# Six edits to an attention, MLP and expert kernel: early decay fills, fp32 partial sums, a fifth block in 128 rows, expert conversions behind the slots

## The chip, the cores and the metric

One NeuronCore of a Trainium2 chip runs the whole kernel. The metric is the device time of one execution in microseconds; lower is better. The engines are TensorE (PE in the profile), VectorE (DVE), ScalarE (ACT), GpSimd (POOL) and SyncE (SP). SP only issues DMAs here; POOL computes a little, issues some DMAs and all gathers and scatters. Each engine takes its instructions in order, so an instruction that waits holds up all that stand behind it on its engine.

## What is computed

Three stages are chained. Attention with a decay term and a causal mask (4 batches, 8 heads, 576 positions, 64 per head), a squared-ReLU MLP over the 2304 tokens, and a mixture of 8 experts of which each token uses two.

```python
scores = np.where(causal, -1e9, q @ k.T / 8 + cum[:, :, :, None] - cum[:, :, None, :])
x = softmax(scores) @ v                         # 4 x 8 x 576 x 64, then (2304, 512)
h = np.maximum(x @ w_in, 0.0)                   # w_in 512 x 2048
x = h * h @ w_out                               # w_out 2048 x 512
noisy = x @ w_gate + np.log1p(np.exp(x @ w_noise)) * noise
# the two largest of 8 per token, softmax of the two as gates
for e in range(8):
    out[mask] += gate * (np.maximum(x[mask] @ w1[e], 0.0) @ w2[e])   # 512 -> 1024 -> 512
```

## The kernel before

Nearly every product is made from fp16 halves: each operand is split into a high and a low fp16 part, and three matmuls (high by high, high by low, low by high) stand for one fp32 product. The splits are work for ACT (high part) and DVE (low part).

**Attention.** The first 256 positions of each batch ("head") are computed in 12 pieces, `hd_s(j, bank)` (L387). A piece fills two PSUM tiles `psab`, one from each half of the 128 rows of the array (z = 0, 1): fp32 products of 64 rows (L398), the decay terms (L403) and the mask (L409). Pieces 0 to 7 are placed by hand; 8 to 11 come from `hd_tick` inside the MLP loop. The other 320 positions ("tail") go in units (batch b, block i, head pair p): scores in `att_s` (L216), the exponential, a split, and `att_pv` (L305), whose probabilities come transposed through DMA. Block i = 4 has only 64 positions. There the two heads of a pair share a PSUM tile (64 columns each), and two kinds of matmul use 64 rows: the mask (L243) and the last of five key blocks in `att_pv` (L323, `K = 64`). There are 16 such units. `prep` (L189) readies the tail's operands in four buffer sets; `make_set` (L173) lets POOL fill the decay rows of a set (`setq`, one memset and two selects, L178 to L180), and `prep` copies three rows of `c16` into `setk` by two DMAs from POOL's queue (L202).

**MLP.** `mm1` (L585, 512 to 2048) and `mm2` (L647, 2048 to 512) run over 6 chunks c of 384 tokens and 16 column blocks i. The weight blocks W[i] arrive as packed words and are unpacked by `conv_w` (DVE L550, L555, L559, ACT L562, DVE L565), so the passes are (c = 0, i 0 to 7), (1, 0 to 7), (0, 8 to 15), (1, 8 to 15), then chunks 2 to 5 whole. Chunks 0 and 1 are therefore left half done: `spill` (L622) writes their PSUM sums `acc` to DRAM as two fp16 halves (ACT, then DVE L626), `unspill` loads them, and `mm2` adds them by two matmuls with `ident2k`, 2048 times the identity (L645), for each of the 3 token tiles.

**Router, slots, experts.** `router` makes the logits of a chunk; `slots` chooses the two experts and a row for each token: a chain of small DVE steps from `lg` (L728) to `si` (L792), then six scatters to `table` on POOL (L795). `slot_rows` reads the rows of an expert back (`tix` on SP, L860, and `gs` on POOL, L862), `gather` fetches their tokens (`xg` on POOL, L871, transposed to `xgT` on SP, L873). `layer1(e)` (L913) and `layer2(e)` (L930) are the expert's two products; its result `y` is scatter-added to the output on POOL (L934). An expert's weights come in 8 loads `wr` of 512 KB on SP into 5 buffers (`fetch_next`), and are split by `split_next` (ACT L835, DVE L836, both 128x1024).

**What sets the order.** A hand-written plan orders all engines up to the first pass of chunk 0. Behind it a scheduler orders each engine's instructions from the program's order and its own estimates; `tc.issue_after(x)` keeps what it encloses behind instruction x.

## Time and profile before

| what | value |
|---|---|
| median of 3 runs | 978.59 us (976.27 to 986.29) |
| the profiled execution | 981.3 us, span of its trace 979.1 us |
| mean granted TensorE clock | 0.983 of full speed |
| PE, DVE, ACT, POOL busy | 944.0, 570.3, 445.6, 209.4 us |
| DMA, mean over the span | 159 GB/s |

The span is the time from the first to the last event of the trace; the execution is 2.2 us longer. Times in rows are microseconds from the span's start unless a column says ns. In a row, `out<-in` names the tiles that an instruction writes and reads, `xN` counts instructions, and `[t <-X]` says that the engine had been idle for t before it and what ended that. The granted clock is a share of TensorE's 2.4 GHz; 0.5 is its lower level of 1.2 GHz.

### The profile page before, as it was taken

The page shows a single profiled execution, that of the slowest core. Times are in us where ns is not written, and L with a number is a line of the kernel's source. Part 1 is how long each engine was busy: PE and PEld are TensorE (multiplying, and loading weights), DVE is VectorE, ACT ScalarE, POOL GpSimd, SP SyncE. Part 2 cuts the span into 40 slices and gives each one's busy share as a digit, 9 for nine tenths or more (in the row PEclk, how much of TensorE's full clock was granted, in tenths as well). Part 3 has the DMA queues.
Part 4 walks back from the last instruction along what each step waited for, and adds up shares of the span by engine and source line. Part 5 has one row for each costly group of instructions (what it writes and reads, how often), then busy time and mean ns, then how long its engine had stood idle before and what let it go on. Part 6 is the DMA issues. An engine that isn't in the chain of part 4 may idle for free.

```text
span 979.1 us, 17623 instructions
## 1 busy us (share of the span) xinstructions
PE 944.0 (96%) x6866; PEld 547.8 (56%) x6866; DVE 570.3 (58%) x1253; ACT 445.6 (46%) x990; POOL 209.4 (21%) x249
## 2 busy tenths in 40 slices
...
GB/s 301 118 242 224 200 149 267 176 215 172 224 156 250 204 89 234 144 55 99 106 332 113 210 37 97 106 219 174 241 144 188 129 194 96 236 82 27 42 12 43
DMA packets 219879, 155.34 MB, mean 159 GB/s; under 512 B 175698, under 2 KB 186322, under 8 KB 217746
## 3 DMA queue, kind: packets, MB, share of 16 engines
...
q10 hardware_dynamic: 144, 0.13, 0.1%
...
## 4 chain that ended last, share of the span: by engine, by line
PE 71%; DMA 8%; issue 7%; DVE 5%; POOL 3%; ACT 2%; SPq 2%; POOLq 0%; DVEq 0%; ACTq 0%
PE e L913 18%; PE e L930 17%; PE m L585 13%; PE acc L647 12%; PE po L320 2%; SPq L873 1%; DMA wr<-in_w_dram 1%; DMA w<-in_w_io_dram 1%; POOL table L795 1%; PE psab L398 1%; PE ps L226 1%; PE ps L227 1%; DMA pt<-phl 1%; PE po L323 1%; DMA xg<-x2d,tix 1%
## 5 line engine op out<-in xcount | busy, mean ns | idle before, releaser
L930 PE MATMUL e<-w2s,hT 128*128 128x512 f16 (+1 forms) x960 | 211.1, 382 | 2.0 <-ACT hT L917 1.3
L913 PE MATMUL e<-xgT,w1s 128*128 128x310 f16 (+2 forms) x1536 | 207.7, 297 | 4.1 <-DMA xgT<-xg 4.1
L647 PE MATMUL acc<-w,g 128*128 128x512 f16 x864 | 205.4, 380 | 0.0
L913 PEld LDWEIGHTS <-w1s 128*128 128x128 f16 x1536 | 140.3, 98 | 70.3 <-issue 8.2
L585 PE MATMUL m<-xT,w 128*128 128x384 f16 x960 | 173.7, 331 | 4.9 <-ACT r L592 3.7
L917 ACT ACTIVATE hT<-e 128x310 f16<-128x310 f32 (+2 forms) x128 | 54.7, 428 | 268.2 <-PE e L913 267.9
L930 PEld LDWEIGHTS <-hT 128*128 128x128 f16 (+1 forms) x960 | 99.8, 104 | 110.1 <-issue 2.2
L585 PEld LDWEIGHTS <-w 128*128 128x128 f16 x1152 | 109.9, 99 | 81.0 <-issue 10.4
L647 PEld LDWEIGHTS <-g 128*128 128x128 f16 x864 | 81.0, 98 | 86.2 <-DVE g L603 0.3
L933 DVE TENSOR_SCALAR y<-e,gs 128x512 f32<-128x512 f32 (+1 forms) x40 | 30.0, 750 | 159.3 <-PE e L930 133.8
L918 DVE SCALAR_TENSOR_TENSOR hT<-e,hT 128x310 f16<-128x310 f32 (+2 forms) x128 | 60.6, 477 | 80.7 <-ACT hT L917 80.4
L934 POOL DMA_INDIRECT out_dram<-y,tix x40 | 65.0, 1625 | 169.6 <-DVE y L933 125.1
L795 POOL DMA_INDIRECT table<-ent,si x36 | 41.4, 1149 | 166.0 <-DVE si L792 156.6
L592 ACT ACTIVATE r<-m 128x384 f32<-128x384 f32 x80 | 39.2, 490 | 68.1 <-PE m L585 67.7
L255 DVE TENSOR_REDUCE sm<-ps 128x1 f32<-128x384 f32 (+2 forms) x96 | 53.1, 562 | 22.1 <-PE ps L243 8.7
L871 POOL DMA_INDIRECT xg<-x2d,tix x40 | 44.3, 1108 | 83.6 <-DMA xgT<-xg 73.3
L258 ACT ACTIVATE pr<-ps,sm 128x384 f32<-128x384 f32 (+1 forms) x64 | 40.2, 630 | 25.8 <-DVE sm L257 23.4
L593 ACT ACTIVATE g<-r 128x384 f16<-128x384 f32 x96 | 50.1, 521 | 3.2 <-PE acc L647 1.5
L836 DVE SCALAR_TENSOR_TENSOR w2s<-wr,w2s 128x1024 f16<-128x1024 f32 x32 | 39.1, 1223 | 19.8 <-ACT w2s L835 19.8
L602 DVE TENSOR_TENSOR r<-r 128x384 f32<-128x384 f32 x64 | 35.4, 553 | 25.2 <-ACT g L593 24.9
L836 DVE SCALAR_TENSOR_TENSOR w1s<-wr,w1s 128x1024 f16<-128x1024 f32 x32 | 39.0, 1225 | 12.7 <-ACT w1s L835 12.5
L279 DVE TENSOR_TENSOR phl<-pr,phl 128x384 f16<-128x384 f32 (+1 forms) x64 | 38.5, 619 | 13.2 <-ACT phl L278 12.8
...
## 6 DMA issues: line engine op xcount, KB each, us to landing
...
```

What stands on the lines that cost most here:

```text
L255: seen[u] = nc.vector.tensor_reduce(sm[:, z:z + 1], ps[z][:, :N], AX.X, ALU.max).ins
L585: nc.tensor.matmul(ps, W[i][:, wi, 0, 128 * cc:128 * cc + 128], xT[:, xi, cc, r0:r0 + CH], start=(x == 0), stop=(x == 11))
L593: nc.scalar.activation(g[:, 0, :], r, AF.Square, scale=2.0 ** -10)
L647: last[0] = nc.tensor.matmul(acc[t], g[:, gi, 128 * t:128 * t + 128], W[i][:, wi, 1, :], start=(i in ends[c][0] and x == 0), stop=(i in en ...
L795: s_ = nc.gpsimd.indirect_dma_start(out=table, out_offset=bass.IndirectOffsetOnAxis(ap=si[:, t, k:k + 1], axis=0), in_=ent[:, t, k, :], in ...
L836: nc.vector.scalar_tensor_tensor(lo, t_, sc, hi, op0=ALU.mult, op1=ALU.subtract)
L871: nc.gpsimd.indirect_dma_start(out=xg, out_offset=None, in_=x2d[0:seen, :], in_offset=bass.IndirectOffsetOnAxis(ap=rows_t[key, j][0], axis=0))
L913: last[0] = nc.tensor.matmul(ps[:, :hw], w1s[:, cc, wi, 128 * i:128 * i + 128], xgT[:, 4 * xi + cc, c], start=(x == 0), stop=(x == 11)).ins
L917: relu[0] = nc.scalar.activation(hi, ps[:, :hw], AF.Relu).ins
L918: nc.vector.scalar_tensor_tensor(hT[:, i, 1, c], ps[:, :hw], 0.0, hi, op0=ALU.max, op1=ALU.subtract)
L930: last[0] = nc.tensor.matmul(ps[:m], hT[:, i, hi, 128 * j:128 * j + m], w2s[:, i, wi, :], start=(i == 0 and x == 0), stop=(i == NFE - 1 an ...
L934: s_ = nc.gpsimd.indirect_dma_start(out=out, out_offset=bass.IndirectOffsetOnAxis(ap=ix[:m], axis=0), in_=y[:m], in_offset=None, compute_o ...
```

## The change

Six edits.

1. **Fills.** The decay rows of the sets 0, 1 and 3 are filled by POOL at the start, behind the constants; set 2 stays where it was. The constant `ident2k` goes.
2. **Partial sums.** `spill` writes one fp32 copy made by ACT; the six DVE steps L626 go. `unspill` is one DMA for a chunk, into the buffer of the packed weights (`w64`). The 12 matmuls L645 go. In `x2_out` of chunks 0 and 1, DVE adds the loaded sums to `acc` (6 new steps of 128x512), and the two steps behind it read SBUF instead of PSUM.
3. **Fifth block.** The mask matmul and the last block of `att_pv` use all 128 rows, also for i = 4 (the rows added are zero).
4. **Head pieces.** From piece 8 on, the matmuls of a piece are chained so that the two row halves take turns.
5. **Rows of slots.** `tix` and `gs` get 8 buffers instead of 6.
6. **Conversions.** In the last chunk, the first five expert weight loads stand behind the first store of chunk 4's result; expert 0's 8 conversions stand behind `si` of the slots of chunk 4, and expert 1's 8 conversions go into `layer1(0)`, one behind each ReLU. Before, 12 of the 16 stood in the last pass and 4 behind it, all before `layer1(0)`.

```diff
@@ -168,3 +168,2 @@
 
-    ident2k = consts.tile([128, 128], F16, name="ident2k")
     ones16 = consts.tile([128, 128], F16, name="ones16")
@@ -174,8 +173,12 @@
         KK[n] = apool.tile([128, 2, 2, S], F16, name=f"setk{n}", tag=f"setk{n}", bufs=1)
+        if n not in QQ:
+            with tc.issue_after(pin["pool"]):
+                make_q(n)
+
+    def make_q(n):
         QQ[n] = apool.tile([128, 2, 2, REST], F16, name=f"setq{n}", tag=f"setq{n}", bufs=1)
         q2 = QQ[n][64:70, 1]
-        with tc.issue_after(pin["pool"]):
-            nc.gpsimd.memset(q2, -8.0)
-            nc.gpsimd.affine_select(q2[:, 0], q2[:, 0], [[0, REST]], ALU.is_ge, 0.0, base=2, channel_multiplier=-1)
-            nc.gpsimd.affine_select(q2[:, 1], q2[:, 1], [[0, REST]], ALU.is_ge, 0.0, base=-3, channel_multiplier=1)
+        nc.gpsimd.memset(q2, -8.0)
+        nc.gpsimd.affine_select(q2[:, 0], q2[:, 0], [[0, REST]], ALU.is_ge, 0.0, base=2, channel_multiplier=-1)
+        nc.gpsimd.affine_select(q2[:, 1], q2[:, 1], [[0, REST]], ALU.is_ge, 0.0, base=-3, channel_multiplier=1)
 
@@ -242,3 +245,3 @@
                         r = slice(64 * z, 64 * z + 64)
-                        nc.tensor.matmul(ps[r, 224:288], identw[0:64, 0:64], maskw[0:64, 0:64], start=False, stop=True, skip_group_check=True)
+                        nc.tensor.matmul(ps[r, 224:288], identw[:, 0:64], maskw[:, 0:64], start=False, stop=True, skip_group_check=True)
 
@@ -316,3 +319,2 @@
             vi, pi = HL3[x]
-            K = 128 if kb < 4 else 64
             first, last = kb == 0 and x == 0, kb == i and x == 2
@@ -322,4 +324,4 @@
             else:
-                nc.tensor.matmul(po[64 * h:64 * h + 64, p // 2, 0, p % 2, :], pt[:K, kb, pi, 64 * h:64 * h + 64],
-                                 vs[:K, kb, h, vi, :], start=first, stop=last, skip_group_check=True)
+                nc.tensor.matmul(po[64 * h:64 * h + 64, p // 2, 0, p % 2, :], pt[:, kb, pi, 64 * h:64 * h + 64],
+                                 vs[:, kb, h, vi, :], start=first, stop=last, skip_group_check=True)
         if p == 3:
@@ -391,2 +393,4 @@
         np_ = 4 // (i + 1)
+        v4 = [t.rearrange("p (c w) -> p c w", w=Wd) for t in ps]
+        prods = []
         for p in range(np_):
@@ -397,4 +401,3 @@
                     r = slice(64 * z, 64 * z + 64)
-                    nc.tensor.matmul(ps[z][:, c], hd["x", b, i][r, 1, pp, :], hd["x", b, kb][r, 0, pp, :],
-                                     start=(p == 0 and kb == 0), stop=False, skip_group_check=True)
+                    prods.append((ps[z][:, c], hd["x", b, i][r, 1, pp, :], hd["x", b, kb][r, 0, pp, :], p == 0 and kb == 0, False))
         for p in range(np_):
@@ -402,5 +405,3 @@
                 r = slice(64 * z, 64 * z + 64)
-                nc.tensor.matmul(ps[z][:, Wd * p:Wd * p + Wd], decay(r, 4 * b + np_ * a + p, 128), c16[r, 0:Wd],
-                                 start=False, stop=False, skip_group_check=True)
-        v4 = [t.rearrange("p (c w) -> p c w", w=Wd) for t in ps]
+                prods.append((ps[z][:, Wd * p:Wd * p + Wd], decay(r, 4 * b + np_ * a + p, 128), c16[r, 0:Wd], False, False))
         for hf in range(2):
@@ -408,4 +409,9 @@
                 r = slice(64 * z, 64 * z + 64)
-                nc.tensor.matmul(v4[z][:, :, 128 * i:128 * i + 128], identb[r, hf], masku[r, hf, None, :].to_broadcast([64, np_, 128]),
-                                 start=False, stop=(hf == 1), skip_group_check=True)
+                prods.append((v4[z][:, :, 128 * i:128 * i + 128], identb[r, hf], masku[r, hf, None, :].to_broadcast([64, np_, 128]), False, hf == 1))
+        prev = None
+        for o_, l_, r_, first, end in prods:
+            with ExitStack() as guard:
+                if j >= NPL and prev is not None:
+                    guard.enter_context(tc.issue_after(prev))
+                prev = nc.tensor.matmul(o_, l_, r_, start=first, stop=end, skip_group_check=True).ins
         if a == 0:
@@ -619,3 +625,3 @@
     ends = [((0, NA), (NA - 1, NF - 1)) if c < 2 else ((0,), (NF - 1,)) for c in range(NCH)]
-    part = dram.tile([2 * CH, 2 * DM], F16, name="part")
+    part = dram.tile([2 * CH, DM], F32, name="part")
 
@@ -623,5 +629,4 @@
         for t in range(NT):
-            sp = gpool.tile([128, 2 * DM], F16, name="sp", tag="x2", bufs=3)
-            nc.scalar.activation(sp[:, :DM], acc[t], AF.Copy, scale=2.0 ** -11)
-            nc.vector.scalar_tensor_tensor(sp[:, DM:], acc[t], 2.0 ** -11, sp[:, :DM], op0=ALU.mult, op1=ALU.subtract)
+            sp = gpool.tile([128, DM], F32, name="sp", tag="x2", bufs=3)
+            nc.scalar.activation(sp, acc[t], AF.Copy)
             nc.sync.dma_start(part[CH * c + 128 * t:CH * c + 128 * t + 128, :], sp)
@@ -631,7 +636,4 @@
     def unspill(c):
-        for t in range(NT):
-            if t % 2 == 0:
-                bk = astream.tile([128, 2, 2 * DM], F16, name="bk", tag="pr", bufs=3)
-            back[t] = bk[:, t % 2, :]
-            nc.sync.dma_start(back[t], part[CH * c + 128 * t:CH * c + 128 * t + 128, :])
+        back[c] = astream.tile([128, NT, DM], F32, name="bk", tag="w64", bufs=2)
+        nc.sync.dma_start(back[c], part[CH * c:CH * c + CH, :].rearrange("(t p) d -> p t d", p=128))
 
@@ -642,5 +644,2 @@
                 acc[t] = psM.tile([128, DM], F32, name=f"acc{t}", tag=f"acc{t}", bufs=1)
-            if i == NA + 4 and c < 2:
-                for z in range(2):
-                    nc.tensor.matmul(acc[t], ident2k, back[t][:, DM * z:DM * z + DM], start=False, stop=False)
             for x, (gi, wi) in enumerate(((0, 0), (0, 1), (1, 0))):
@@ -650,2 +649,4 @@
     x2T_t = {}
+    x2_put = [None]
+    slotted = [None]
 
@@ -655,7 +656,11 @@
             x2T = gpool.tile([128, 8, 128], F16, name="x2T", bufs=3)
-            nc.scalar.activation(x2[:, :DM], acc[t], AF.Copy, scale=2.0 ** -10)
-            nc.vector.scalar_tensor_tensor(x2[:, DM:], acc[t], 2.0 ** -10, x2[:, :DM], op0=ALU.mult, op1=ALU.subtract)
+            src = acc[t]
+            if c < 2:
+                src = back[c][:, t]
+                nc.vector.tensor_tensor(src, acc[t], src, op=ALU.add)
+            nc.scalar.activation(x2[:, :DM], src, AF.Copy, scale=2.0 ** -10)
+            nc.vector.scalar_tensor_tensor(x2[:, DM:], src, 2.0 ** -10, x2[:, :DM], op0=ALU.mult, op1=ALU.subtract)
             r0 = SPARE + CH * c + 128 * t
             nc.sync.dma_start_transpose(out=x2T, in_=x2)
-            nc.sync.dma_start(x2d[r0:r0 + 128, :], x2)
+            x2_put[0] = nc.sync.dma_start(x2d[r0:r0 + 128, :], x2).ins
             x2T_t[t] = x2T
@@ -791,3 +796,3 @@
         nc.vector.tensor_reduce(sf, sl, AX.X, ALU.add)
-        nc.vector.tensor_copy(si, sf)
+        slotted[0] = nc.vector.tensor_copy(si, sf).ins
         for t in range(NT):
@@ -858,5 +863,5 @@
         rows = slice(r0, r0 + 128 * n) if row is None else bass.ds(row, 128)
-        tix = epool.tile([128, NJ, 2], I32, name="tix", bufs=6)
+        tix = epool.tile([128, NJ, 2], I32, name="tix", bufs=8)
         nc.sync.dma_start(tix[:, :n, :].rearrange("p j w -> p (j w)"), table[rows, :].rearrange("(p j) w -> p (j w)", p=128))
-        gs = epool.tile([128, NJ], F32, name="gs", bufs=6)
+        gs = epool.tile([128, NJ], F32, name="gs", bufs=8)
         nc.gpsimd.tensor_scalar(gs[:, :n], tix[:, :n, 1].bitcast(F32), 2.0 ** -25, None, op0=ALU.mult)
@@ -1024,5 +1029,7 @@
             nc.gpsimd.memset(half[64:128], 1.0)
-            for t_, cmp, val in ((identw, ALU.not_equal, 1.0), (maskw, ALU.is_ge, -BIG), (ident2k, ALU.not_equal, 2048.0)):
+            for t_, cmp, val in ((identw, ALU.not_equal, 1.0), (maskw, ALU.is_ge, -BIG)):
                 nc.gpsimd.memset(t_, 0.0)
-                pin["pool"] = nc.gpsimd.affine_select(t_, t_, [[-1, 128]], cmp, val, base=0, channel_multiplier=1).ins
+                nc.gpsimd.affine_select(t_, t_, [[-1, 128]], cmp, val, base=0, channel_multiplier=1)
+            for n in (0, 1, 3):
+                make_q(n)
         elif tok[0] == "X" and tok[1] != "T":
@@ -1155,6 +1162,7 @@
         if (c, i) == (NCH - 1, 2):
-            for _ in range(WR):
-                fetch_next()
-        if c == NCH - 1 and i >= 4:
-            split_next()
+            with tc.issue_after(x2_put[0]):
+                for _ in range(WR):
+                    fetch_next()
+        if c == NCH - 1 and 4 <= i < 12:
+            split_next(slotted[0])
         if (c, i) == (NCH - 1, 5):
@@ -1172,6 +1180,10 @@
     ov = ctx.enter_context(tc.tile_pool(name="ov", bufs=1, side="left"))
-    while at["split"] < 16:
-        split_next()
     lastp = []
-    layer1(0, 0, NE0, lambda i: lastp.append(router(NCH - 1, (psE, "e2", 2, 512), last[0])) if i == NR1 else None, last[0])
+
+    def begin(i):
+        split_next(relu[0])
+        if i == NR1:
+            lastp.append(router(NCH - 1, (psE, "e2", 2, 512), last[0]))
+
+    layer1(0, 0, NE0, begin, last[0])
     layer2(0, 0, NE0, lambda j: slots(NCH - 1, lastp[0], (psE, "e2", 2, 512), last[0]) if j == 0 else None)
```

What it moves on the engines is seen at three places (line numbers before and after differ by some: L202 is L205, L795 is L800, L728 is L733, L836 is L841, L398 to L409 are all L416).

On POOL, at about 210 to 235 us: the copies into the four `setk` sets and the first six scatters to `table`. Before:

```order
L202 DMA setk0_1635<-c16_84 3x2x576 x2
L285 MEMSET ph4_2690 128x2x64
L285 MEMSET ph4_2785 128x2x64
L202 DMA setk1_1653<-c16_84 3x2x576 x2
L795 DMA table_82<-ent_2518,si_2550 19456x2 x6
L202 DMA setk2_1719<-c16_84 3x2x576 x2
L202 DMA setk3_1786<-c16_84 3x2x576 x2
```

After:

```order
L205 DMA setk0_1636<-c16_84 3x2x576 x2
L288 MEMSET ph4_2670 128x2x64
L205 DMA setk1_1650<-c16_84 3x2x576 x2
L288 MEMSET ph4_2759 128x2x64
L205 DMA setk2_1712<-c16_84 3x2x576 x2
L800 DMA table_82<-ent_2498,si_2530 19456x2 x6
L205 DMA setk3_1779<-c16_84 3x2x576 x2
```

The copy into set 2 now stands ahead of the six scatters; only that into set 3 is left behind them.

On DVE, the beginning of the chain of `slots` for chunk 4, with the conversions (`w1s`, `w2s`) and the MLP's `r` and `g`. Before:

```order
L728 TENSOR_SCALAR lg<-pl 128x48
L603 SCALAR_TENSOR_TENSOR g<-r,g 128x384
L836 SCALAR_TENSOR_TENSOR w2s<-wr,w2s 128x2x512
L733 TENSOR_SCALAR u__6773<-e__6772 128x24
L736 TENSOR_SCALAR d__6778<-u__6773 128x24
L836 SCALAR_TENSOR_TENSOR w2s<-wr,w2s 128x2x512
L737 TENSOR_TENSOR e__6772<-e__6772,d__6778 128x24
L738 RECIPROCAL u__6773<-u__6773 128x24
L836 SCALAR_TENSOR_TENSOR w2s<-wr,w2s 128x2x512
L739 TENSOR_TENSOR e__6772<-e__6772,u__6773 128x24
L602 TENSOR_TENSOR r<-r 128x384
L740 TENSOR_TENSOR l__6774<-l__6774,e__6772 128x24
```

After:

```order
L733 TENSOR_SCALAR lg<-pl 128x48
L738 TENSOR_SCALAR u__6750<-e__6749 128x24
L741 TENSOR_SCALAR d__6755<-u__6750 128x24
L742 TENSOR_TENSOR e__6749<-e__6749,d__6755 128x24
L743 RECIPROCAL u__6750<-u__6750 128x24
L744 TENSOR_TENSOR e__6749<-e__6749,u__6750 128x24
L745 TENSOR_TENSOR l__6751<-l__6751,e__6749 128x24
L746 TENSOR_TENSOR l__6751<-l__6751,nz 128x24
L748 TENSOR_TENSOR nl<-l__6751,lg 128x24
L752 MAX m_6764<-nl 128x8 x3
L753 MAX_INDEX i_6765<-m_6764,nl 128x8 x2
```

The conversions have left the chain; no conversion stands between `lg` and `si` any more (before, twelve), and four stand right behind `si`.

On PE, the products of head piece 11 (`psab`, two tiles, one for each row half). Before, one half of it, with the other half a hundred rows further on:

```order
L398 MATMUL psab_1304<-hraw_203,hraw_677 128x128
L398 MATMUL psab_1304<-hraw_677 128x128
L398 MATMUL psab_1304<-hraw_203,hraw_677 128x128
L398 MATMUL psab_1304<-hraw_677 128x128
L403 LDWEIGHTS esel_92
L403 MATMUL psab_1304<-c16_84,esel_92 128x256
```

After, both halves (their first product stands 47 rows ahead of these):

```order
L416 MATMUL psab_1309<-hraw_210,hraw_684 128x128
L416 MATMUL psab_1308<-hraw_684 128x128
L416 MATMUL psab_1309<-hraw_684 128x128
L416 MATMUL psab_1308<-hraw_210,hraw_684 128x128
L416 MATMUL psab_1309<-hraw_210,hraw_684 128x128
L416 MATMUL psab_1308<-hraw_684 128x128
L416 MATMUL psab_1309<-hraw_684 128x128
L416 LDWEIGHTS esel_92
L416 MATMUL psab_1308<-c16_84,esel_92 128x256
```

The tiles now alternate, 1205 and 1206, where before one tile's four products followed each other.

## Rows read from the trace of the kernel before

**Rows 1.** The page: busy time of each engine, its share of the span, instructions.
```profile
PE 944.0 (96%) x6866; PEld 547.8 (56%) x6866; DVE 570.3 (58%) x1253; ACT 445.6 (46%) x990; POOL 209.4 (21%) x249
```

**Rows 2.** Windows: stretch, length, busy time of PE, PEld, DVE, ACT, POOL, PEclk, DMA, GB/s.
```profile
100.00:120.00 20.00, 20.00 (x156) 11.90 (x155) 19.16 (x34) 14.84 (x39) 3.21 (x12) 1.00 0.85 177
...
140.00:160.00 20.00, 16.34 (x82) 8.26 (x81) 18.13 (x21) 16.00 (x26) 7.75 (x10) 0.91 0.54 179
...
260.00:480.00 220.00, 220.00 (x2007) 122.15 (x2006) 166.22 (x469) 132.85 (x318) 37.89 (x52) 1.00 0.72 150
```

**Rows 3.** Two waits of PE: what waited, for what, total us, times, longest.
```profile
PE ps L227 <- DMA setk<-c: 1.4, 1, 1.4
...
PE e L930 <- ACT hT L917: 1.3, 1, 1.3
```

**Rows 4.** The chain that ended last, 170 to 175 us: start, us, what.
```profile
172.21 0.43 PE acc L645 x2
```

**Rows 5.** Timeline of PE at 301 us, a unit of block 4: start, us, instructions.
```profile
301.15 0.32 PE L237 MATMUL ps<-setk,setq 128*64 128x288 f16 x2
301.30 0.29 PE L239 MATMUL ps<-setk,setq 70*64 70x288 f16 x2
301.52 0.21 PE L243 MATMUL ps<-maskw,identw 64*64 64x64 bf16 x2
301.67 0.78 PE L323 MATMUL po<-vs,pt 128*64 128x64 f16 x30
302.38 0.61 PE L647 MATMUL acc<-w,g 128*128 128x512 f16 x2
```

**Rows 6.** Timeline of PE, head pieces: halves in turn, and one half alone.
```profile
51.42 1.16 PE L398 MATMUL psab<-hraw 64*128 64x128 f32 x16
52.41 0.39 PE L403 MATMUL psab<-c,esel 64*128 64x256 f16 x4
...
93.35 1.16 PE L398 MATMUL psab<-hraw 64*128 64x128 f32 x8
94.34 0.38 PE L403 MATMUL psab<-c,esel 64*128 64x256 f16 x2
```

**Rows 7.** Timeline of DVE, 134 to 147 us: unpacking a weight block, and a spill.
```profile
134.91 1.17 DVE L550 TENSOR_SCALAR w<-w 128x1024 int32<-128x1024 int32 x1 [1.57 <-DMA w<-in_w_io_dram]
...
136.72 1.46 DVE L555 SCALAR_TENSOR_TENSOR w<-w,w 128x1024 int32<-128x1024 int32 x1
...
145.36 1.27 DVE L626 SCALAR_TENSOR_TENSOR sp<-acc,sp 128x512 f16<-128x512 f32 x2
```

**Rows 8.** The page's costliest groups: an expert conversion on DVE, count, busy, mean ns.
```profile
L836 DVE SCALAR_TENSOR_TENSOR w2s<-wr,w2s 128x1024 f16<-128x1024 f32 x32 | 39.1, 1223 | 19.8 <-ACT w2s L835 19.8
```

**Rows 9.** Timeline of POOL: decay fills, scatters to the table, copies into sets.
```profile
133.19 2.34 POOL L178 MEMSET setq<- 6x640 f16 x4
...
142.94 1.42 POOL L180 TENSOR_SCALAR_AFFINE_SELECT setq<-setq 6x320 f16<-6x320 f16 x1
...
222.73 2.76 POOL L795 DMA_INDIRECT table<-ent,si  x1 [11.90 <-DVE si L792]
...
233.24 2.31 POOL L202 DMA_DIRECT2D setk<-c  x4
```

**Rows 10.** Timeline of PE: the start, two stalls, and the undisturbed layer1.
```profile
8.30 0.61 PE L403 MATMUL psab<-c,esel 64*128 64x128 f16 x8 [0.95 <-DVE c L147]
...
144.31 3.69 PE L585 MATMUL m<-xT,w 128*128 128x384 f16 x12 [3.26 <-ACT r L592]
...
551.51 8.75 PE L913 MATMUL e<-xgT,w1s 128*128 128x512 f16 x27 [4.11 <-DMA xgT<-xg]
...
564.63 5.34 PE L913 MATMUL e<-xgT,w1s 128*128 128x512 f16 x24
```

**Rows 11.** Timeline of DVE: the slots of chunk 4 are known.
```profile
525.25 0.16 DVE L792 CAST si<-sf 128x6 int32<-128x6 f32 x1
```

**Rows 12.** Timeline of SP: the rows of an expert are asked for.
```profile
682.55 0.34 SPq L860 DMA_DIRECT2D tix<-table  x1
```

## The prediction, made before the changed kernel was run

> **What bounds the kernel now.** I read the page first, then the windows, then PE's waits, and last the timelines around each wait. PE is busy for 944.0 of the 979.1 us of the span [rows 1], so every saving must either take work from PE or close one of its few gaps. The windows say which of the two holds where. From 260 to 480 us PE is busy for all of the 220 us [rows 2]: work taken away there counts in full, and faster helpers bring nothing. From 100 to 120 us PE is full as well, but DVE has 19.16 us of work in 20; from 140 to 160 us PE has only 16.34 while DVE has 18.13, and the granted clock is 0.91 on average [rows 2], which means that PE ran at the lower level (1.2 GHz) for a while after standing idle, a loss of 20 x 0.09 = 1.8 us on top of the gap. So that stretch is bound by DVE, the only one in the middle that is.
>
> The waits behind it are short and far between. PE stood 3.26 us at 144 us for the ReLU of a first-layer tile and 4.11 us at 551 us for the first expert's tokens [rows 10], 1.4 us for the decay rows of a set and 1.3 us for a hidden tile of expert 1 [rows 3]. A stall costs more than its length: the 27 matmuls that began at 551.51 took 8.75 us, where 24 later ones take 5.34 [rows 10], so 27 x 5.34 / 24 = 6.0; the clock took 2.7 us more, 6.8 in all.
>
> **The change, part by part.**
>
> *Partial sums, PE.* Two of the removed L645 take 0.43 us on the chain that ended last [rows 4]. There are 3 tiles x 2 halves x 2 chunks = 12: **-2.6**. PE is nearly always busy where they stood, so I count all. The six adds that replace them are DVE work of 128x512, about 0.64 us each by the spill's two in 1.27 [rows 7]. They free `acc` after the add and come at the end of a pass, with the other passes' matmuls queued on PE: nothing, at most +1 if the next pass waits for `acc`.
>
> *Fifth block.* The change of form costs time. In a unit of block 4 the step from L237 to L239 is 0.15 us, from L239 to the 64-row L243 it is 0.22 [rows 5]: 0.07 more. The 30 matmuls L323 last 0.71 us until L647; only the last six of them use 64 rows, and no row shows the other 24 alone. What the six cost beyond their share is therefore between 0 and half of that time, 0.35; a change of form into them is one such 0.07 at least, and a second one may come at their end, so I take 0.13. With 0.07 that is 0.20 in each of 16 units: **-3.3**, between -1.1 and -6.7.
>
> *Head pieces.* Sixteen records with halves in turn take from 51.42 to 52.41, 0.99 us; eight of one half alone take from 93.35 to 94.34, also 0.99 [rows 6]. So two halves one after the other cost twice what they cost in turns. For four pieces that is 4.0 us of products and, with the narrower decay and mask terms, perhaps 5. But the order cuts a piece differently: its first product stands alone, the other seven 47 rows on, and each new group pays a change of form as above. I take **-3.0**, from 0 to -5. The pieces lie around 93 us, where PE is full or nearly so, ahead of the stall at 144.
>
> *Spill and fills, 100 to 160 us.* Six DVE steps of 0.64 us go, 3.8 us, half of them (chunk 0's) ahead of the stall at 144 and half in it [rows 7]. POOL's fills ran from 133.19 to 144.4 [rows 9], just over the unpacking of a weight block. There a two-operand step of 128x1024 took 1.46 us [rows 7], where the expert conversion, also of two operands and 128x1024, takes 1.22 on average [rows 8]; some eight steps ran beside the fills, 8 x 0.24 = 1.9 us. After the change one set of four is filled there. DVE's chain is thus shorter by about 1.9 ahead of the stall, by 1.9 in it and by 1.5 for the fills, 5.3, against a stall of 3.26 and 1.8 of clock. But PE arrives up to 3 us earlier too (head pieces), and the weight loads that feed DVE (it waited 1.57 us for one [rows 7]) need not come sooner. I take **-3.0**, from 0 to -7.
>
> *Decay rows.* POOL began the six scatters at 222.73 and the four copies behind them at 233.24 [rows 9]; PE waited 1.4 us for such a copy [rows 3]. The order now has set 2's copies ahead of the scatters. **-1.5**, from 0 (PE then waits for set 3) to -3.3 with a clock loss like that at 144.
>
> *Slots of chunk 4.* The rows of chunk 4 are known at 525.25 [rows 11]; PE stands ready at 551.51 - 4.11 = 547.40 and goes on at 551.51 [rows 10], so the chain from `si` over the scatters, `tix`, the gather and its transposes takes 26.3 us. The order shows twelve conversions between `lg` and `si` before and none now: 12 x 1.22 = 14.6 us [rows 8] by DVE alone. Needed are 4.1. What can eat the rest is SP: seven weight loads, which wait for buffers that the now later conversions free, stand ahead of the `tix` loads; seven conversions at 1.22 are 8.5 us. 14.6 - 8.5 = 6.1 remains, more than 4.1. The stall goes with its clock loss, 6.8. What is late next: four conversions right behind `si` hold DVE 4.9 us, and `r` and `g` of the last MLP blocks stand behind them; PE has a block or two in hand, I allow it 0.8. **-6.0**, from 0 to -6.8. Expert 1's conversions now run in `layer1(0)`, one to each step of 12 matmuls; PE needs 5.34 us for 24 [rows 10], so 2.67 for a step, and DVE gets 1.22 more in each [rows 8]: PE hides them. Without that cover eight would cost 9.8.
>
> *Rows of slots.* SP asked for an expert's rows only at 682.55 [rows 12], when the scatter that read the buffer was done. Weight loads stand behind it on SP, a conversion behind them on ACT, and `hT` behind that, for which PE waited 1.3 us [rows 3]. Two more buffers let SP ask one expert sooner. With a clock loss like 1.8 that is **-3.0**, from 0 to -3.5.
>
> *Start.* POOL fills three sets from about 7.6 us; by the 11.2 us for four that is 8.4 us, beside DVE's first steps, for which PE waits (0.95 us at 8.30 [rows 10]). Some four steps on the path stretched by 0.24 each: **+1.0**, from 0 to +2. Set 2's fill is later as before.
>
> Two operands matter there: beside selects of up to 1.42 us [rows 9] the two-operand step was only 0.24 us longer [rows 7, 8], so it was slowed and did not wait out a whole select. If two steps on the start's path did wait one out, that would be 2 x 1.42 = 2.8 instead of 1.0, a rival below. The Trainium skill speaks for that rival, in "SBUF — State Buffer", section "Who interferes with whom": a DVE instruction with two SBUF inputs and a GpSimd instruction that reads SBUF exclude each other, and the loser blocks for the whole instruction. By that rule the sum would be 1.8 less of a gain; by the row it stays.
>
> The sum: -2.6 - 3.3 - 3.0 - 3.0 - 1.5 - 6.0 - 3.0 + 1.0 = **-21.4**. Against the profiled execution that is 979.1 - 21.4 = 957.7 of span, and 981.3 - 21.4 = 959.9 of time. That execution lies 2.7 above the median of 978.59, so against the median I say **957.2 us**, 2.2% less.
>
> **The rivals.**
>
> *A, absorbed.* Around the stall at 144 us the weight loads pace DVE, and DVE paces PE. Then what PE saves ahead (head pieces) is waited away at the next block, and the spill's steps go without gain: 957.2 + 3.0 + 3.0 = 963.2. For it: DVE waited for a load [rows 7]. Against it: DVE is at 96% in 100 to 120 us [rows 2], and the stretched steps lie on its chain.
>
> *B, the conversions' new place.* The four conversions behind `si` hold up `g`; PE waits for up to 4.9 us and loses 2.7 of clock, 7.6 instead of the 0.8 allowed: 964.0. For it: in the order they stand in one piece. Against it: DVE is otherwise lightly loaded there.
>
> *C, slower.* In the new order of POOL the gathers for the second next expert stand ahead of some scatters of the present one. A gather waits for its `xgT` buffer; if scatters behind it come late, the results' three buffers fill up, DVE cannot empty PSUM, and PE stops in each of the experts 2 to 7. With a stall s and 2.7 of clock each: 957.2 + 6 (s + 2.7). It takes s above 2.5 us to make the kernel slower by 1%; with the 4.11 of 551 us it would be 998. Against it: the buffer comes free when `layer1` of the expert ends, and only then do its scatters begin.
>
> *D, the start waits.* Two DVE steps on the start's path each wait out a whole select, as worked out above: 2.8 instead of 1.0, so 959.0. For it: PE waits for such a step at 8.30 us [rows 10]. Against it: the 0.24 us beside the fills.
>
> **How the numbers follow.** Chances: the forecast 0.50, A 0.18, B 0.14, C 0.07, D 0.11. The likeliest is 957.2; its own range, with the bounds of the terms not all at one end, is 947 to 964. A with B gives 970, so the range is 946 to 971, with C and a few mishaps left out. A measurement of this kernel can tell about 1% from no change, here 968.8 to 988.4. Faster than that: the forecast, A and D nearly whole, B mostly: 0.78. Within: 0.16, for A with B, or for the slots' and the tix terms failing together. Slower: 0.06, most of C.
>
> **What would show it.** Right if PE's waits no longer list the expert's tokens, `r` falls well under 3 us in all, the clock between 140 and 160 us and between 550 and 600 us reads 1.00, and PE stays full from 260 to 480 us, with the last attention unit some 2 us earlier against its neighbours. A shows as waits of DVE for weight loads with PE waiting at 120 to 170 us; B as waits of PE for `g` after 500 us; C as waits in the experts at regular steps of some 50 us; D as a later first `psab`. The forecast falls if PE has new gaps in 250 to 540 us, where it had none.

## The result, and the profile after

| kernel | median, us | runs | ratio to before, 95% interval |
|---|---|---|---|
| before | 978.09 | 22 | |
| the change | 968.01 (960.78 to 979.53) | 22 | 0.9895 [0.9874, 0.9916] |

The medians lie 10.1 us apart, where 21.4 were forecast. By the ratio, which leaves out the executions that ran in a slower state, the change gains 10.3 us, 1.05%. The time lies inside the range of 946 to 971, and that is luck: the range goes beyond 964 only for the rivals A and B together, and B didn't come. Less than half of the gain of 21.4 us is there. The profiled execution of the changed kernel took 971.0 us, with a span of 969.1 and a mean granted clock of 0.992.

Lines moved with the change: L398 to L409 are now L416, L515 is L521, L502 is L508, L585 and L592 are L591 and L598, L647 is L646, L728 and L792 are L733 and L797, L913 to L918 are L918 to L923, L930, L933 and L934 are L935, L938 and L939. (The tiles that take turns in the order of head piece 11 are `psab_1308` and `psab_1309`.)

The page's busy times, to be held against [rows 1]:

```profile
PE 930.8 (96%) x6854; PEld 541.4 (56%) x6854; DVE 568.3 (59%) x1253; ACT 445.5 (46%) x990; POOL 202.8 (21%) x247
```

PE is busy for 13.2 us less, but the span is only 10.0 shorter: PE now stands idle for 38.3 us instead of 35.1. Part of the work taken away came back as waiting. Not all of the 13.2 us belongs to the change: the first 52 us ran at a mean granted clock of 0.87 in the execution before and 1.00 in this one, which differs between executions of one program too (last section). The waits of PE (for what; total us, times, longest) say where:

```profile
PE po L521 <- DMA pt<-phl: 7.3, 2, 4.2
...
PE m L591 <- ACT r L598: 3.7, 5, 1.9
...
PE e L935 <- DVE y L938: 3.0, 1, 3.0
PE psab L416 <- DVE c L147: 1.3, 1, 1.3
```

and, of the kernel before:

```profile
PE m L585 <- ACT r L592: 3.7, 2, 3.3
```

The wait for the expert's tokens and the one for the decay rows of a set are gone from the list, as forecast. New at the top are two waits for `pt`, the probabilities of the head pieces, transposed through DMA; `r`, which was to fall well under 3 us, stands at 3.7 as before; and in the experts a wait for `y` has come. In windows (stretch, length, busy PE, PEld, DVE, ACT, POOL, PEclk, DMA, GB/s):

```profile
100.00:120.00 20.00, 15.82 (x113) 8.79 (x113) 18.04 (x31) 12.64 (x33) 2.46 (x13) 0.93 0.73 159
120.00:140.00 20.00, 20.00 (x151) 11.77 (x150) 16.09 (x23) 10.44 (x23) 4.64 (x5) 0.92 0.75 195
140.00:160.00 20.00, 18.10 (x120) 9.81 (x119) 14.59 (x21) 16.78 (x28) 3.44 (x6) 1.00 0.67 205
...
540.00:590.00 50.00, 50.00 (x267) 23.19 (x265) 25.27 (x65) 15.56 (x24) 10.97 (x12) 1.00 0.57 140
...
640.00:690.00 50.00, 46.86 (x284) 28.78 (x283) 22.72 (x32) 14.86 (x25) 13.79 (x12) 0.97 0.88 202
```

Against [rows 2], the gap and the low clock have moved from 140 to 160 us to 100 to 140 us. Between 140 and 160 us DVE became lighter, 14.59 us instead of 18.13, and PE fuller, 18.10 instead of 16.34; but between 100 and 120 us, where PE had been full, it now lacks 4.18 of 20. The stretch from 540 to 590 us, where the first expert had stood, is full and at full clock; a hole has opened at 640.

The timeline of PE at the start and at these places:

```profile
8.55 0.61 PE L416 MATMUL psab<-c,esel 64*128 64x128 f16 x8 [1.26 <-DVE c L147]
...
99.46 0.45 PE L521 MATMUL po<-vh,pt 128*128 128x64 f16 x5 [3.13 <-DMA pt<-phl]
...
119.34 0.23 PE L521 MATMUL po<-vh,pt 128*128 128x64 f16 x2 [4.18 <-DMA pt<-phl]
...
543.33 15.70 PE L918 MATMUL e<-xgT,w1s 128*128 128x512 f16 x72
...
644.71 7.03 PE L935 MATMUL e<-w2s,hT 128*108 128x512 f16 x24 [3.04 <-DVE y L938]
```

Expert 0 now begins at 543.33 without a wait; before, PE was ready at 547.40 and went on at 551.51 [rows 10]. In expert 1 PE stands for 3.04 us and then takes 7.03 us for 24 matmuls; the same 24 take 5.34 where the wait is short (the kernel with 6 buffers, below), so 1.7 more went at the lower clock.

### The profile page after: what moved, and what is told of

Read it like the earlier page. It is cut to its first block, busy times and chain, and to the rows that moved or that the text cites. A ratio compares the mean times of both kernels' runs of the same rounds, so it can differ in the third digit from the quotient of the medians.

```text
span 969.1 us, 17580 instructions
## 1 busy us (share of the span) xinstructions
PE 930.8 (96%) x6854; PEld 541.4 (56%) x6854; DVE 568.3 (59%) x1253; ACT 445.5 (46%) x990; POOL 202.8 (21%) x247
## 4 chain that ended last, share of the span: by engine, by line
PE 78%; DMA 12%; DVE 5%; issue 2%; ACT 2%; POOL 1%; SPq 0%; POOLq 0%; ACTq 0%; DVEq 0%
PE e L918 19%; PE e L935 18%; PE acc L646 15%; PE m L591 13%; DMA pt<-phl 5%; PE m1s L591 3%; PE po L322 2%; DMA out_dram<-y,tix 2%; PE psab L416 1%; DMA vr<-in_v_dram 1%; DMA qkr<-in_qk_dram 1%; PE ps L229 1%; PE ps L230 1%; DMA w<-in_w_io_dram 1%; PE po L325 1%
## 5 line engine op out<-in xcount | busy, mean ns | idle before, releaser
L935 PE MATMUL e<-w2s,hT 128*128 128x512 f16 (+1 forms) x960 | 211.2, 381 | 3.1 <-DVE y L938 3.0
L646 PE MATMUL acc<-w,g 128*128 128x512 f16 x864 | 206.7, 381 | 0.3 <-DVE g L609 0.2
L918 PE MATMUL e<-xgT,w1s 128*128 128x310 f16 (+2 forms) x1536 | 204.7, 294 | 0.0
L918 PEld LDWEIGHTS <-w1s 128*128 128x128 f16 x1536 | 139.7, 97 | 63.9
L591 PE MATMUL m<-xT,w 128*128 128x384 f16 x960 | 170.5, 326 | 4.9 <-ACT r L598 3.7
L935 PEld LDWEIGHTS <-hT 128*128 128x128 f16 (+1 forms) x960 | 100.2, 105 | 110.9 <-issue 5.0
L591 PEld LDWEIGHTS <-w 128*128 128x128 f16 x1152 | 108.8, 98 | 78.8 <-issue 7.6
L646 PEld LDWEIGHTS <-g 128*128 128x128 f16 x864 | 81.7, 98 | 87.9 <-issue 2.2
L938 DVE TENSOR_SCALAR y<-e,gs 128x512 f32<-128x512 f32 (+1 forms) x40 | 30.0, 751 | 164.9 <-PE e L935 116.0
L923 DVE SCALAR_TENSOR_TENSOR hT<-e,hT 128x310 f16<-128x310 f32 (+2 forms) x128 | 60.2, 477 | 60.2 <-ACT hT L922 58.0
L939 POOL DMA_INDIRECT out_dram<-y,tix x40 | 64.9, 1622 | 140.4 <-DVE y L938 132.8
L876 POOL DMA_INDIRECT xg<-x2d,tix x40 | 41.4, 1034 | 128.9 <-DMA xgT<-xg 121.0
L800 POOL DMA_INDIRECT table<-ent,si x36 | 41.0, 1140 | 130.1 <-DVE si L797 120.6
L598 ACT ACTIVATE r<-m 128x384 f32<-128x384 f32 x80 | 38.9, 486 | 59.6 <-PE m L591 56.9
L841 DVE SCALAR_TENSOR_TENSOR w2s<-wr,w2s 128x1024 f16<-128x1024 f32 x32 | 39.1, 1222 | 17.7 <-ACT w2s L840 17.6
L840 ACT ACTIVATE w2s<-wr 128x1024 f16<-128x1024 f32 x32 | 33.7, 1052 | 29.4 <-DMA wr<-in_w_dram 28.7
```

Of the source, the lines that this page charges most:

```text
L591: nc.tensor.matmul(ps, W[i][:, wi, 0, 128 * cc:128 * cc + 128], xT[:, xi, cc, r0:r0 + CH], start=(x == 0), stop=(x == 11))
L646: last[0] = nc.tensor.matmul(acc[t], g[:, gi, 128 * t:128 * t + 128], W[i][:, wi, 1, :], start=(i in ends[c][0] and x == 0), stop=(i in en ...
L800: s_ = nc.gpsimd.indirect_dma_start(out=table, out_offset=bass.IndirectOffsetOnAxis(ap=si[:, t, k:k + 1], axis=0), in_=ent[:, t, k, :], in ...
L876: nc.gpsimd.indirect_dma_start(out=xg, out_offset=None, in_=x2d[0:seen, :], in_offset=bass.IndirectOffsetOnAxis(ap=rows_t[key, j][0], axis=0))
L918: last[0] = nc.tensor.matmul(ps[:, :hw], w1s[:, cc, wi, 128 * i:128 * i + 128], xgT[:, 4 * xi + cc, c], start=(x == 0), stop=(x == 11)).ins
L923: nc.vector.scalar_tensor_tensor(hT[:, i, 1, c], ps[:, :hw], 0.0, hi, op0=ALU.max, op1=ALU.subtract)
```

## The experiments

Ratios are to the kernel before. What "brings nothing" means is limited by the intervals, some 3 to 4 us to either side.

**Where the gain comes from.** First edits 1 to 3 alone: from the changed kernel, the turns, the 8 buffers and the new place of the conversions are undone.

```diff
-                if j >= NPL and prev is not None:
+                if False:
-        tix = epool.tile([128, NJ, 2], I32, name="tix", bufs=8)
+        tix = epool.tile([128, NJ, 2], I32, name="tix", bufs=6)
-            with tc.issue_after(x2_put[0]):
-                for _ in range(WR): fetch_next()
-        if c == NCH - 1 and 4 <= i < 12: split_next(slotted[0])
+            for _ in range(WR): fetch_next()
+        if c == NCH - 1 and i >= 4: split_next()
```

(and `gs` like `tix`, and expert 1's conversions back out of `layer1(0)`)

> Edits 1, 2 and 3 alone: the head pieces as before, 6 buffers for the rows of slots, the conversions as before. Theory: what counts in full is PE's own work (partial sums 2.6 and fifth block 3.3 to 4.2), the shorter chain of DVE and the earlier fills bring nothing, and the stall for expert 0's tokens stays: 6 to 7 us under the kernel before, 0.993 to 0.994. Rival, that the front waits away even this work: 0.997 to 1.000. Rival, the forecast as it stood (2.6 + 3.3 + 3.0 + 1.5 - 1.0 = 9.4): 0.990.

Measured: 973.52 us, 0.9931 [0.9904, 0.9958], so 6.7 us less. That is what PE's own work gives and hardly more. I added up, for every matmul of a kind, the time from its start to the next start (at most 0.15 us over the kind's median, so that waits don't count):

```
us of PE                        before   this kernel   whole change
L645, 12 adds of partial sums     2.59      0             0
block 4 (scores, mask, values)   26.68     22.43         22.79
```

2.6 + 4.2 = 6.8 by this kernel's 22.43 (2.6 + 3.9 = 6.5 by the 22.79 of the whole change). The forecast's other terms for these edits, -3.0 for spill and fills, -1.5 for decay rows and +1.0 for the start, would have made 9.4 by its sum; that is the edge of the interval, so the time alone doesn't exclude them. The stretch that they were to fill speaks against them. In windows as above:

```profile
140.00:160.00 20.00, 15.61 (x77) 7.70 (x75) 13.58 (x20) 15.13 (x24) 3.43 (x6) 0.91 0.74 242
```

DVE has 4.55 us less to do than in [rows 2], 13.58 instead of 18.13, and PE is no fuller: 15.61 instead of 16.34.

Then edit 6 alone, put into the kernel before:

```diff
-            for _ in range(WR): fetch_next()
-        if c == NCH - 1 and i >= 4: split_next()
+            with tc.issue_after(x2_put[0]):
+                for _ in range(WR): fetch_next()
+        if c == NCH - 1 and 4 <= i < 12: split_next(slotted[0])
```

(and expert 1's conversions into `layer1(0)`, as in the change)

> The kernel before with edit 6 alone (expert weight loads and conversions behind the slots). If edit 6 is what closes both PE's wait for the first tokens (4.1 us and 2.7 us of clock) and, without the longer ring, the wait for expert 1's hidden tile (about 4 us with its clock loss): 968 us, as the whole change. Rival: it closes the first alone: 972 us.

Measured: 972.93 us, 0.9943 [0.9917, 0.9970], 5.6 less: the forecast's 6.0. The reverse, the whole change with edit 6 undone:

```diff
-        if c == NCH - 1 and 4 <= i < 12:
-            split_next(slotted[0])
+        if c == NCH - 1 and i >= 4:
+            split_next()
```

(and the weight loads and expert 1's conversions back to where they were)

> The changed kernel with the expert conversions and weight loads where they were (edit 6 undone). If edit 6 is worth what PE's wait for the first tokens cost, 4.1 us and 2.7 us at half clock come back: about 975 us. Rival: edit 6 also made the wait for y in expert 1 (about 4.7 us with the clock), which then goes: about 970 us.

Measured: 972.75 us, 0.9963 [0.9934, 0.9991]; the whole change loses 6.7 of its 10.3 us by this (0.9963 against 0.9895). Of PE's waits of this kernel:

```profile
PE e L935 <- DVE y L938: 5.5, 1, 5.5
...
PE e L918 <- DMA xgT<-xg: 3.7, 1, 3.7
```

The wait for expert 0's tokens is back with 3.7 us, near the 4.11 of before [rows 10], so edit 6 is what takes it away. The edit moves weight loads as well as conversions, and no run parts the two. But DVE's chain from `lg` to `si` shows what the conversions do. In this kernel, and in the whole change:

```profile
485.98 0.21 DVE L733 TENSOR_SCALAR lg<-pl 128x48 f32<-128x48 f32 x1
...
515.22 0.16 DVE L797 CAST si<-sf 128x6 int32<-128x6 f32 x1
```

```profile
488.95 0.21 DVE L733 TENSOR_SCALAR lg<-pl 128x48 f32<-128x48 f32 x1 [0.53 <-PE pl L729]
...
501.55 0.17 DVE L797 CAST si<-sf 128x6 int32<-128x6 f32 x1
```

29.2 us with twelve conversions in between, which take 14.6 of it, and 12.6 without them. Over all the traces the chain takes 29.0 to 29.6 us with the conversions at their old place (six executions) and 12.5 to 13.1 at their new one (nine).

Last, edits 1, 2, 3 and 6 without 4 and 5:

```diff
-                if j >= NPL and prev is not None:
+                if False:
-        tix = epool.tile([128, NJ, 2], I32, name="tix", bufs=8)
+        tix = epool.tile([128, NJ, 2], I32, name="tix", bufs=6)
```

> Edits 1, 2, 3 and 6 without 4 and 5. Theory: the turns and the two more buffers bring nothing in time, so this kernel is as fast as the whole change, 0.987 to 0.991, with no stall for expert 0's tokens, no stall of 3 us for y in expert 1 and the old one for hT in its place. Rival, the forecast's terms for both (3.0 + 3.0) real: 6 us slower than the whole change, 0.995 to 0.997. Rival, that the two edits cost time: 0.983 to 0.986.

Measured: 968.93 us, 0.9892 [0.9854, 0.9929], the same as the whole change with its 0.9895. The turns and the two buffers, for which 6.0 us were forecast, bring nothing. What PE waits for without them:

```profile
PE e L935 <- ACT hT L922: 6.5, 1, 6.5
...
PE po L521 <- DMA pt<-phl: 1.5, 1, 1.5
```

Against the list of the whole change, `pt` is down from 7.3 to 1.5 us, `y` is gone, and `hT` has 6.5. It looks as if each of the two edits trades one wait for another; the next two groups of runs try that.

**The turns.** Undone alone:

```diff
-                if j >= NPL and prev is not None:
+                if False:
```

> The changed kernel without edit 4 (head pieces 8 to 11 not chained). Order theory: the chain put PE's products with the head's probabilities nearer to the transposes that feed them; without it the two waits of PE for the transposes (7.3 us in all in the changed kernel) fall below 2 us and the time to about 962 us. Absorption theory: PE comes to these products sooner because of what it saved before, and the transposes land no sooner, whatever the order of the pieces; the waits stay at 5 us or more, less what PE now spends more on the pieces, and the time stays within 2 us of the changed kernel's 968.

Measured: 965.74 us, 0.9872 [0.9839, 0.9906]: nothing is lost. Then the turns alone, put into the kernel before:

```diff
+                if j >= NPL and prev is not None:
+                    guard.enter_context(tc.issue_after(prev))
```

> The kernel before with edit 4 alone (head pieces 8 to 11 in turns). As predicted: 3 us less, 975 us. Absorption: PE spends some 5 us less on the four pieces in the trace and waits as much longer for transposes or first-layer tiles before 160 us; the time is 977 to 980 us.

Measured: 979.87 us, 1.0010 [0.9983, 1.0037]: nothing is gained. Yet they do what they say. The late pieces (80 products, 20 decay terms and 20 masks, from start to next start, at most 0.6 us each) take:

```
us of PE          halves apart                       halves in turn
before            13.4     this edit alone            9.9
edits 1 to 3      13.4     whole change              10.5
turns undone      14.7     conversions undone         9.5
```

So PE saves 3 to 5 us of work, as forecast, and waits for most of it again: the wait for `pt<-phl` (L521) is 0.9 to 2.3 us in six executions without the turns, 1.9 on average, and 2.9 to 7.6 in six that have them (with the products at this place), 4.7 on average (7.3 in the whole change). PE's row in the kernel with the turns alone:

```profile
98.04 1.46 PE L519 MATMUL po<-vh,pt 128*128 128x64 f16 x24 [3.12 <-DMA pt<-phl]
```

In the kernel without the turns that product begins at 99.96 us, in the whole change at 99.46; in a second execution of the unchanged kernel at 101.0. In all four it waits for the landing of the transposed probabilities, and the landing comes only 0.5 us sooner by the turns in the whole change.

If that wait is the gate, then to place these products one piece later should free the gain:

```diff
-        if NPL <= j - 2 < NSUB:
-            hd_pv16(j - 2)
+        if NPL <= j - 3 < NSUB:
+            with tc.issue_after(last[0]):
+                hd_pv16(j - 3)
```

(the sums behind them and the range of `j` move along, here and in the two kernels below with this edit)

> The changed kernel with the products of head pieces 8 to 11 with their probabilities placed one step later (three steps behind the scores instead of two, and behind the second-layer matmuls issued by then), about 8 us of PE work later for the first piece. If the landing of the transposes near 99 us is the gate that takes back what PE saves ahead of it, PE's first wait (3.1 us in the changed kernel) and its clock loss of 1.7 us go and the time falls by 4 us or more, to 964 or less. Rival: the next gate (unpacking of the weights, ACT's r) takes that back too, and the time stays within 2 us of 968.

Measured: 965.49 us, 0.9868 [0.9836, 0.9900]. The wait at 99 us is gone, but its length stands at the next piece, where PE waits for a transpose that lands when that of the second wait in the whole change did:

```profile
119.37 0.45 PE L521 MATMUL po<-vh,pt 128*128 128x64 f16 x5 [7.32 <-DMA pt<-phl]
```

The same placing in the kernel before, where there is little wait to remove:

```diff
-            hd_pv16(j - 2)
+            with tc.issue_after(last[0]):
+                hd_pv16(j - 3)
```

> The kernel before with the same placing of the products one step later, without any of the six edits. If the gate belongs to both kernels, it gains like the changed kernel, 2 to 4 us (its waits at 98 to 101 us were 0 to 2.5 us with up to 5 us of clock): 974 to 976 us. Rival: the gate matters only for the changed kernel, which comes there earlier: 978 us and more.

Measured: 977.78 us, 1.0003 [0.9975, 1.0031]. The placing is worth nothing there, and with the turns perhaps 2.5 us (965.49 against 968.01, intervals that overlap). That speaks for the transposes, and not PE's order, as what sets this stretch. What holds a transpose is seen on SP, in the whole change and in the kernel without the turns:

```profile
106.01 11.21 SPq L508 DMA_TRANSPOSE pt<-phl  x1
```

```profile
104.36 1.32 SPq L508 DMA_TRANSPOSE pt<-phl  x1
105.84 6.79 SPq L695 DMA_DIRECT2D table<-ini  x2
```

SP is held for 11.21 us in the issue of one transpose, that on which PE waits until 119.34. Without the turns the same instruction takes 1.32 us, and the two writes to `table` behind it hold SP for 6.79. In the whole change these two writes stood ahead of it (104.89), and POOL had started weight loads at 102.99 and 107.99. So the next kernel moves the `table` writes out of the way:

```diff
-        if (n, i) == (1, 1):
+        if (n, i) == (2, NA + 3):
             router_setup()
```

> The changed kernel with the router's setup (among it the three writes that initialise the table of slots, on SP) moved from the second step of chunk 1's first pass to a late step of chunk 0's second pass. If these writes hold up the transposes behind them on SP (one took 11.2 us to issue), that wait of 4.2 us and its 1.7 us at half clock go: about 962 us. Rival: the 1 MB weight loads in flight hold them up, and the time stays within 2 us of 968.

Measured: 973.87 us, 0.9937 [0.9913, 0.9962], slower than the whole change by 4 us (by the ratios). The second wait for `pt` is gone, and others are there:

```profile
PE acc L646 <- DVE g L607: 4.9, 2, 4.2
PE psxf L479 <- DVE xs L339: 3.2, 2, 2.3
...
PE po L521 <- DMA pt<-phl: 2.9, 1, 2.9
```

The long issue itself is gone as well, though weight loads still start around it (105.11 and 110.31):

```profile
107.76 3.11 SPq L508 DMA_TRANSPOSE pt<-phl  x1
```

It takes 3.01 to 3.11 us in this kernel and the two below that write the table later, and 4.4 to 11.2 in four with the writes right ahead of it. So the writes have their part in it, and a weight load alone doesn't make it; why they hold it for so long is not settled. Yet nothing is gained, since PE then waits elsewhere: what one edit frees in this stretch another wait takes.

One more profiled execution of the unchanged kernel, to see how much of [rows 10] belongs to the kernel and how much to one execution:

> The kernel before, profiled once more, to see how far its waits ahead of 250 us differ from one execution to the next. If the front's waits are a matter of the order alone, the same ones come back within 1 us of their length; if the transfers decide, PE's idle time ahead of the last MLP block differs by several us, as it did between two kernels that have the same front.

Measured: 982.66 us (one execution). There the stall for `r` at 144 us, on which the forecast put 3.0 us, is short:

```profile
146.59 2.11 PE L585 MATMUL m<-xT,w 128*128 128x384 f16 x12 [1.23 <-ACT r L592]
```

1.23 us and full clock behind it, where [rows 10] have 3.26. The wait for the tokens is the same (4.20 against 4.11). So the stall at 551 belongs to the kernel, and the length of the one at 144 to one execution. The stretch isn't without idle time for that:

```profile
100.00:120.00 20.00, 19.02 (x112) 11.02 (x113) 12.96 (x24) 10.76 (x25) 2.49 (x12) 0.74 0.51 129
...
140.00:160.00 20.00, 16.99 (x92) 8.77 (x91) 18.09 (x21) 14.57 (x23) 10.68 (x13) 1.00 0.47 164
```

Between 140 and 160 us PE lacks 3.0 of 20 (3.7 in [rows 2]), in three short waits instead of a long and a short one, and the low clock lies between 100 and 120 us, where [rows 2] have 1.00.

**Rows of slots.** The whole change with 6 buffers:

```diff
-        tix = epool.tile([128, NJ, 2], I32, name="tix", bufs=8)
+        tix = epool.tile([128, NJ, 2], I32, name="tix", bufs=6)
-        gs = epool.tile([128, NJ], F32, name="gs", bufs=8)
+        gs = epool.tile([128, NJ], F32, name="gs", bufs=6)
```

> The changed kernel with 6 buffers for tix and gs instead of 8 (edit 5 undone). Theory that the ring moved the stall: PE's wait for y in expert 1 (3.0 us and 1.7 us at half clock) comes from gathers that the longer ring put ahead of a scatter on POOL; it goes, and the wait for the expert's rows and weights of the kernel before (about 4 us with its clock loss) comes back: within 1.5 us of the changed kernel. Rival: the wait for y comes from the conversions' new place and stays, and the old one comes back on top: about 972 us.

Measured: 969.31 us, 0.9899 [0.9858, 0.9940], the same as with 8. What the longer ring does is seen in expert 1. With 8 buffers, DVE (`y`), POOL (gathers `xg`, scatters to `out_dram`) around the first and the fourth `y`:

```profile
622.02 0.75 DVE L938 TENSOR_SCALAR y<-e,gs 108x512 f32<-108x512 f32 x1
...
643.91 0.75 DVE L938 TENSOR_SCALAR y<-e,gs 128x512 f32<-128x512 f32 x1 [10.67 <-DMA out_dram<-y,tix]
```

```profile
627.75 0.95 POOL L876 DMA_INDIRECT xg<-x2d,tix  x1 [3.43 <-DMA xgT<-xg]
629.36 0.95 POOL L876 DMA_INDIRECT xg<-x2d,tix  x1 [0.66 <-issue]
630.62 1.65 POOL L939 DMA_INDIRECT out_dram<-y,tix  x1 [0.31 <-issue]
```

And with 6, the same places:

```profile
623.23 0.74 DVE L938 TENSOR_SCALAR y<-e,gs 108x512 f32<-108x512 f32 x1
...
642.29 0.75 DVE L938 TENSOR_SCALAR y<-e,gs 128x512 f32<-128x512 f32 x1 [7.88 <-DMA out_dram<-y,tix]
```

```profile
627.54 0.95 POOL L876 DMA_INDIRECT xg<-x2d,tix  x1 [3.27 <-DMA xgT<-xg]
628.80 1.64 POOL L939 DMA_INDIRECT out_dram<-y,tix  x1 [0.31 <-issue]
```

`y` has three buffers; the fourth `y` of the expert needs the first one's scatter to have landed. With 8 buffers POOL knows more rows and makes one gather more ahead of that scatter. The scatter leaves 8.6 us after its `y` (622.02 to 630.62), with 6 buffers 5.6 (623.23 to 628.80). The 3.0 us between them come through to PE: it waits 3.04 us for `y` with 8 buffers, and with 6:

```profile
643.09 5.34 PE L935 MATMUL e<-w2s,hT 128*108 128x512 f16 x24 [0.25 <-DVE y L938]
```

So this wait comes from the ring. In all five kernels with 8 buffers PE waits for `y` in expert 1, 1.3 to 5.5 us, and never for ACT's `hT`. In nine of the ten executions with 6 buffers it waits for `hT`, 0.8 to 6.5 us, and for `y` 1.1 at most. The tenth is the one just measured: its trace has neither wait, and its time is still that of the whole change; the interval is too wide to tell what 3 us less would do. The next two kernels have 6 buffers and write the table four steps of the MLP later, the second with the head's products later too:

```diff
-        if (n, i) == (1, 1):
+        if (n, i) == (1, 5):
             router_setup()
```

> The changed kernel with 6 buffers for tix and gs, and with the router's setup (with the three writes that initialise the table of slots) four steps later, in the sixth step of chunk 1's first pass. Theory that these writes and a weight load in flight hold up the transposes of a head piece on SP: PE's second wait for such transposes (4.2 us, and its 1.7 us at half clock) goes, nothing new comes at 150 us, as it did where the setup stood still later; with no wait for y in expert 1 the time is about 960 us. Rival: the transposes of another piece are held up instead, and the time stays at 966 to 969 us.

Measured: 968.05 us, 0.9898 [0.9863, 0.9933]. The second wait for `pt` is gone and that for `y` nearly (0.4 us); the first for `pt` is 4.0 us, and the one for `hT` is back:

```profile
PE e L935 <- ACT hT L922: 3.0, 1, 3.0
```

The third edit on top, as in the experiment on the head's products:

```diff
-            hd_pv16(j - 2)
+            with tc.issue_after(last[0]):
+                hd_pv16(j - 3)
```

> The changed kernel with 6 buffers for tix and gs, the router's setup four steps later, and the products one step later. If gate, table writes and ring each cost what the runs before showed (4 us, 3 to 5 us in some executions, 1 to 2 us): about 960 us, faster than both kernels. Rival: the waits move on, 966 us.

Measured: 968.33 us, 0.9902 [0.9868, 0.9936], with 3.8 us of waiting for `hT`. No combination beats the change by more than its interval; the lowest times are those without the turns and those with the head's products later, 965.7 and 965.5.

## Why the prediction was wrong, and where it was right

Three steps failed: that what PE saves in the head pieces counts, that DVE sets the stretch from 140 to 160 us, and that a longer ring just takes a stall away. Their terms were 3.0 us each, and together they brought about nothing.

*Partial sums, -2.6: right.* The twelve matmuls took 2.59 us, and nothing took their place.

*Fifth block, -3.3: right in the sum, 3.9, and in part by luck.* The split was the wrong way round. From the timeline of a unit after:

```profile
297.82 0.32 PE L242 MATMUL ps<-setk,setq 70*64 70x288 f16 x2
297.94 0.22 PE L246 MATMUL ps<-maskw,identw 128*64 128x64 bf16 x2
```

From L242 to the mask L246 it is now 0.12 us, where it was 0.22 [rows 5]. Over the 16 units the scores and the mask went from 14.58 to 11.78 us, the values only from 12.10 to 11.02. The forecast put 0.13 of its 0.20 on the values.

*Slots of chunk 4, -6.0: right,* 5.6 alone. The slots are known at 501.55 us, 23.7 earlier than in [rows 11], 16.8 of them by the shorter chain of DVE (29.4 to 12.6), where the forecast counted 14.6. The four conversions behind them hold DVE as allowed for:

```profile
502.11 4.68 DVE L841 SCALAR_TENSOR_TENSOR w1s<-wr,w1s 128x1024 f16<-128x1024 f32 x4 [0.40 <-issue]
```

PE stayed full from 510 to 590 us, so rival B fell.

*Head pieces, -3.0: the step that failed is that what PE saves there counts.* PE's work fell by about that, but the pieces' own probabilities come back over a transpose that lands hardly sooner (99.46 us against 99.96), and the wait for it is 7.3 us with the turns and 2.3 without. The prediction looked for the wait one stage on, at 144 us, and read "PE is full or nearly so" around 93 us as if PE alone set the time there. That PE is full only shows that nothing makes it wait yet; a chain just behind it is not seen in the windows. That work saved ahead is waited away is what rival A said (0.18), but at another place and for another reason: the transposes of `pt`, not the weight loads.

*Spill and fills, -3.0: the step that failed is that DVE sets the stretch from 140 to 160 us; decay rows, -1.5; start, +1.0.* DVE's chain did get shorter, and the two-operand step did lose its stretch:

```profile
137.94 1.22 DVE L561 SCALAR_TENSOR_TENSOR w<-w,w 128x1024 int32<-128x1024 int32 x1
```

It took 1.46 before [rows 7]. The wait for decay rows went from 1.4 to nothing. But of 3.5 us in sum, the kernel with edits 1 to 3 shows nothing (6.7 less the 6.8 of PE's work), within about 2.7 either way. With 4.55 us less of DVE's work PE is no fuller there. It still waits for `r`, which is ACT's, and in the whole change that is seen to have a reason of its own:

```profile
146.00 1.15 ACT L199 ACTIVATE setk<-qkr 128x1152 f16<-128x1152 f32 x1
...
150.61 0.47 ACT L598 ACTIVATE r<-m 128x384 f32<-128x384 f32 x1
...
151.13 2.11 PE L591 MATMUL m<-xT,w 128*128 128x384 f16 x12 [1.90 <-ACT r L598]
```

PE's product for this `r` was done at 146.3, but from 146.00 to 150.61 ACT makes six copies in one piece, which ready operands for the tail (`setk`, `setq`, `vs`, twice), and `r` stands behind them. In the kernel with edits 1 to 3 the same six copies stand ahead of one `r` (PE waits 1.45 us), and ahead of the next stands a `setk` that waited 3.74 us for its load (PE waits 1.95). The prediction looked at DVE's load in this stretch and not at ACT's order. The base was weak too: 3.0 us were read off a stall of 3.26 us of one execution, which was 1.23 in another execution of the same program; `r` costs 3.7 us in all before and after. The start cost 0.25 us (8.55 against 8.30 in [rows 10]; 8.44 to 8.58 in ten kernels with the fills, 8.18 to 8.30 in five without). That is a quarter of the +1.0, and rival D, with two whole selects waited out, fell. DVE's two-operand step at the start, and the select of POOL beside it:

```profile
7.89 0.61 DVE L147 SCALAR_TENSOR_TENSOR c<-c,pm,fch 128x256 f16<-128x256 f16 x1
```

```profile
7.78 0.45 POOL L182 TENSOR_SCALAR_AFFINE_SELECT setq<-setq 6x320 f16<-6x320 f16 x1
...
131.54 2.30 POOL L182 TENSOR_SCALAR_AFFINE_SELECT setq<-setq 6x320 f16<-6x320 f16 x1
```

The step takes 0.13 us more than the 0.48 of before. The Trainium skill, "SBUF — State Buffer", section "Who interferes with whom", states that a DVE instruction with two SBUF inputs contends with a GpSimd instruction that reads SBUF. The trace agrees that the two disturb each other. At the start DVE didn't wait out the 0.34 us that were left of the select, though POOL's times are rough; at 131.54 it is POOL that is held, 2.30 us for a select of the same size, beside DVE steps of two operands from 131.11 to 133.54.

*Rows of slots, -3.0: the failed step is that the stall just goes.* It goes, and POOL's extra gather brings one of 3.04 us and 1.7 of clock in its place. That is rival C's mechanism (0.07), in one expert instead of six: behind 690 us PE has no wait that would show it. What spoke against C, that the buffer `xgT` comes free before the scatters begin, does not hold in expert 1: there a gather of POOL's waited 3.43 us (at 627.75) for a transpose that still read `xg`.

In sum: 6.7 (edits 1 to 3) + 5.6 (edit 6) + about nothing for 4 and 5 = 12.3, against a measured 10.3 [8.2, 12.3] by the ratio (10.6 for edits 1, 2, 3 and 6 in one kernel). The two intervals of the parts are 2.7 us wide to each side, so the 2 us left over lie within the noise, and no run explains them.
